# Forward and backward of four attention layers on one core: the derivative of the linear layers' feature map, recomputed on GpSimd from the kept feature map in place of being stored and loaded

## The chip, the core and the metric

One core of a Trainium2 chip runs the whole program in one launch. The metric is the time of one execution in device microseconds; the kernel before was run three times. A profile of one more execution gives, per engine, every instruction's start and length, the DMA transfers and the clock that TensorE was granted. The engines are called PE (TensorE, matmuls), PEld (its weight loads), DVE (VectorE), ACT (ScalarE), POOL (GpSimd) and SP (SyncE, which here only issues DMAs). ACT issues DMAs too, in the same in-order queue as its computing instructions.

## The reference, cut to what matters

The input x is 2048 tokens of 640 numbers in bfloat16. Four layers follow each other: linear attention (A), sliding-window attention (B, window 256), A, B, each with a layer norm ahead, a residual sum behind, 32 heads of 20 numbers, and weights wqkv (640x1920) and wo (640x640). The two A layers share their weights, and so do the two B layers. Outputs are the result and the gradients of x and of the four weights for a given grad_out.

```python
phi = lambda t: jnp.where(t > 0, t + 1, jnp.exp(t)) + 1e-6
pq, pk = phi(q), phi(k)
kv = jnp.einsum("bhsd,bhse->bhde", pk, v)
z = jnp.einsum("bhsd->bhd", pk)
num = jnp.einsum("bhqd,bhde->bhqe", pq, kv)
den = jnp.einsum("bhqd,bhd->bhq", pq, z)[..., None] + 1e-6
o = num / den
```

This is the A layer's inner part. For the backward the derivative of phi is needed: 1 where t > 0, and exp(t) elsewhere, that is min(exp(t), 1). Since phi(t) is max(t, 0) + min(exp(t), 1) + 1e-6, the same derivative can be had from phi itself as min(phi - 1e-6, 1).

## The kernel before

The tokens are cut into 16 tiles of 128 rows (TT = 16); layers are numbered 0 to 3. What the backward needs of an A layer is kept in HBM: pq and pk (phi of q and k), eq and ek (the derivatives, min(exp(t), 1)), v, o, the reciprocal denominators and the small matrix of kv.

The work goes through these stages, with about the times at which they run in the profile:

- First pass, to 120 us: layer 0's layer norm and q, k, v of every tile (`a_qkv`, lines 488 to 538). Each chunk of 320 columns is five matmuls (L448), an exponential on ACT into the tile `ee` (L516), a minimum with 1 on DVE (L517), and on DVE max(t, 1e-6) + ee into pq or pk (L520; pk lies in `gcar`). The v chunks are copied by ACT (L501) or DVE (L504). The transposes of the normalized input and of pq are done by PE (L464) and copied by ACT (L467). ACT issues the stores of pq, eq, pk, ek and v of the tile, 160 KB each (all DMAs of the forward have line 416).
- First combined pass, to about 420 us: per tile layer 0's output, layer 1 (the B layer, scores L826, exponentials L830 and L833 on ACT, masks L839 and L844 on POOL, the products with v L864, copies of q, k, v L695, reciprocal and output L871 and L872), and layer 2's k and v. ek of layer 2 is stored here.
- Second combined pass, about 460 to 745 us: layer 2's q (`late_q`, lines 542 to 569, begun at 420 us), its output, and layer 3. eq of layer 2 is stored here, by line 569.
- Backward of layer 3's attention, to about 1045 us (`B_attn_bwd`), whose order is written out by hand.
- A phase to about 1440 us (`bwd_phase(3, 2, 1)`): first a loop that ends layer 3's backward and starts layer 2's (gw L1327 and prod L1418 on POOL), then from 1235 us a loop over 16 tiles with layer 2's gradients of q, k and v (`lin_grads`, lines 1465 to 1508), its layer-norm backward (`tail`, L1309 to L1331) and the start of layer 1's (`local_dO`, with prod L1377 on POOL).
- Layer 1's attention backward to about 1780 us, then `bwd_phase(1, 0, None)` to the end, whose gradient loop over the tiles runs from 1965 to 2070 us and has no `local_dO`.

In `lin_grads` a tile's `start` issues on SP three transposing loads (dNT, pkT, vT) and the plain loads of eq and ek (L1476, through `load`, L1227; the issue itself is on L1128). Each of the two tiles has two buffers; in the phase of layers 3 and 2 ek lies in a part of `slabR`, so the profile calls it slabR there. `chunk` then does the banded matmuls (L1145) and, for q and k, DVE multiplies the PSUM result by eq or ek into dqkv (L1503), 320 columns at a time. dqkv is transposed by PE (L1167), copied by DVE (L1171) and multiplied by the weights (L1138, dw_ps); ACT copies the result (dh, L1309), DVE reduces it (L1317), ACT makes w (L1324), POOL adds the running gradient (gw, L1327), and DVE writes the new running gradient (gcar, L1329).

In the forward and in `bwd_phase` the order of the instructions of each engine is set ahead of the run by a planner (`Sched`, lines 87 to 200). Each operation is given to `op` with its engine, an assumed duration and the tiles that it reads and writes; the planner places them one after the other by when they could start by its own model, and each engine's queue is then fixed. A DMA counts with its size and a short time for the issue. So an operation that is taken out or added can change the order of others on every engine. On the chip each engine works through its queue in order and waits where an operand isn't ready.

Of the kernel before, what the change touches and what calls it, by code (L numbers as in the profile page):

```python
# [10 lines left out]
ACT = mybir.ActivationFunctionType  # L11
ALU = mybir.AluOpType
AX = mybir.AxisListType
BF = mybir.dt.bfloat16
# [188 lines left out]
class Kern:  # L203
    def __init__(self, ctx, tc, x0, A_wqkv, A_wo, B_wqkv, B_wo, grad_out, outs):
# [5 lines left out]
        D, T = self.D, self.T  # L210
# [59 lines left out]
        d = self.dram  # L270
        self.hn_d = [d.tile([T, D], BF, name=f"hn{l}") for l in range(4)]
        self.sv = {}
        for l in (0, 2):
            self.sv[l] = dict(
                pq=d.tile([T, D], BF, name=f"pq{l}"), pk=d.tile([T, D], BF, name=f"pk{l}"),
                eq=d.tile([T, D], BF, name=f"eq{l}"), ek=d.tile([T, D], BF, name=f"ek{l}"),
                v=d.tile([T, D], BF, name=f"v{l}"), o=d.tile([T, D], BF, name=f"o{l}"),
                r32=d.tile([T, self.H], F32, name=f"r32{l}"),
                mbd=d.tile([D, D + P], BF, name=f"mbd{l}"),
            )  # L280
# [53 lines left out]
    def forward(self, slabs):  # L334
# [5 lines left out]
        with ExitStack() as st:  # L340
# [36 lines left out]
            pk = g = self.g  # L377
# [32 lines left out]
            op = S.op  # L410
            dq = dict(SP=nc.sync, ACT=nc.scalar)

            def dma(eng, out, in_, size, r, w, **kw):
                def f():
                    with nc.allow_non_contiguous_dma(reason="strided layouts"):
                        dq[eng].dma_start(out=out(), in_=in_())
                op(eng, 60, f, r, w, dma=("D", size), **kw)
# [19 lines left out]
            KB = 1024  # L437
# [50 lines left out]
            def a_qkv(l, tt, hnT):  # L488
                sv = self.sv[l]
                c = {}  # L490

                def chunk(ci):
                    def f():
                        kind, c0 = "qkv"[ci // 2], ci * CW
                        o = c0 - ci // 2 * D
                        ps = R["s" if l == 0 and ci in (0, 2, 4) else "mm"].buf()
                        mm_chunk(ps, CW, [(lambda k=k: hnT.t[:, k, :], lambda k=k: wsb["Wqkv_A"][:, k, c0:c0 + CW],
                                           k == 0, k == DT - 1) for k in range(DT)], [key_of(hnT), ("Wqkv_A", ci)])
                        if kind == "v":
                            if ci == 4 and l == 0:  # L500
                                op("ACT", av(CW), lambda: nc.scalar.copy(vv[:, tt, o:o + CW], ps.t[:, 0:CW]), [ps],  # L501
                                   [("vv", tt, ci)])
                            else:
                                op("DVE", vp(CW), lambda: nc.vector.tensor_copy(vv[:, tt, o:o + CW], ps.t[:, 0:CW]),  # L504
                                   [ps], [("vv", tt, ci)])
                            if ci == 5:
                                dma("ACT", lambda: self.tm_view(sv["v"])[:, tt, :], lambda: vv[:, tt, :], 160 * KB,
                                    [("vv", tt, 4), ("vv", tt, 5)], [])
                            return
                        if ci % 2 == 0:  # L510
                            c[kind] = R["ee"].buf()
                            if kind == "q":
                                c["p"] = R["pp"].buf()
                        e = c[kind]
                        es = lambda: e.t[:, o:o + CW]
                        op("ACT", av(CW), lambda: nc.scalar.activation(es(), ps.t[:, 0:CW], ACT.Exp), [ps], [(e, ci)])  # L516
                        op("DVE", v4(CW), lambda: nc.vector.tensor_scalar(  # L517
                            out=es(), in0=es(), scalar1=1.0, scalar2=None, op0=ALU.min), [], [(e, ci)])
                        pd = (lambda: c["p"].t[:, o:o + CW]) if kind == "q" else (lambda: pk[:, tt, o:o + CW])
                        op("DVE", vp(CW), lambda: nc.vector.scalar_tensor_tensor(  # L520
                            out=pd(), in0=ps.t[:, 0:CW], scalar=1e-6, in1=es(), op0=ALU.max,
                            op1=ALU.add), [ps, (e, ci)], [(c["p"], ci) if kind == "q" else ("pk", tt, ci)])
                        if ci == 3 and "q" in c:
                            p_, e = c["p"], c["q"]
                            turn("s", lambda: pqT[:, :, tt * P:(tt + 1) * P], lambda: p_.t, DT, [(p_, 0), (p_, 1)],
                                 [("pqT", tt)])
                            dma("ACT", lambda: self.tm_view(sv["pq"])[:, tt, :], lambda: p_.t, 160 * KB,
                                [(p_, 0), (p_, 1)], [])
                            dma("ACT", lambda e=e: self.tm_view(sv["eq"])[:, tt, :], lambda e=e: e.t, 160 * KB,
                                [(e, 0), (e, 1)], [])  # L530
                        if ci == 3:
                            e = c["k"]
                            dma("ACT", lambda: self.tm_view(sv["pk"])[:, tt, :], lambda: pk[:, tt, :], 160 * KB,
                                [("pk", tt, 2), ("pk", tt, 3)], [])
                            dma("ACT", lambda e=e: self.tm_view(sv["ek"])[:, tt, :], lambda e=e: e.t, 160 * KB,
                                [(e, 2), (e, 3)], [])
                    return f
                return [chunk(ci) for ci in range(6)]

# [2 lines left out]
            def late_q(l, tt, where="s1", **F):  # L542

                sv = self.sv[l]
                q_left.discard(tt)
                e, p_ = R["ee"].buf(), R["pp"].buf()
                own = lambda: pqT[:, :, tt * P:(tt + 1) * P]
                for ci in range(2):
                    ps, c0 = R[where].buf(), ci * CW
                    for k0, k1 in ((0, 2), (2, DT)):  # L550
                        def f(ps=ps, c0=c0, k0=k0, k1=k1):
                            for k in range(k0, k1):
                                nc.tensor.matmul(ps.t[:, 0:CW], lhsT=own()[:, k, :], rhs=wsb["Wqkv_A"][:, k, c0:c0 + CW],
                                                 start=(k == 0), stop=(k == DT - 1))
                        op("PE", pe([CW] * (k1 - k0)), f, [("pqT", tt), ("Wqkv_A", ci)], [ps], **F)
                    es = lambda c0=c0: e.t[:, c0:c0 + CW]
                    op("ACT", av(CW), lambda ps=ps, es=es: nc.scalar.activation(es(), ps.t[:, 0:CW], ACT.Exp), [ps],
                       [(e, ci)], **F)
                    op("DVE", v4(CW), lambda es=es: nc.vector.tensor_scalar(out=es(), in0=es(), scalar1=1.0, scalar2=None,
                                                                            op0=ALU.min), [], [(e, ci)], **F)  # L560
                    op("DVE", vp(CW), lambda ps=ps, es=es, c0=c0: nc.vector.scalar_tensor_tensor(
                        out=p_.t[:, c0:c0 + CW], in0=ps.t[:, 0:CW], scalar=1e-6, in1=es(), op0=ALU.max, op1=ALU.add),
                       [ps, (e, ci)], [(p_, ci)], **F)
                if tt < 2:
                    turn("mm", own, lambda: p_.t, DT, [(p_, 0), (p_, 1)], [("pqT", tt)])
                else:
                    flip(own, lambda: p_.t, 160 * KB, [(p_, 0), (p_, 1)], [("pqT", tt)], **F)
                dma("ACT", lambda: self.tm_view(sv["pq"])[:, tt, :], lambda: p_.t, 160 * KB, [(p_, 0), (p_, 1)], [], **F)
                dma("ACT", lambda: self.tm_view(sv["eq"])[:, tt, :], lambda: e.t, 160 * KB, [(e, 0), (e, 1)], [], **F)

            def a_kv(l):
                sv = self.sv[l]
# [518 lines left out]
    def bwd_phase(self, lb, la, nb, ahead, raw):  # L1091
# [9 lines left out]
        with ExitStack() as st:  # L1101
# [125 lines left out]
            def load(name, src, tt):  # L1227
                b = R[name].buf()
                dma("SP", lambda: b.t, lambda: self.tm_view(src)[:, tt, :], 160 * KB, [], [b])
                return b  # L1230
# [234 lines left out]
            def lin_grads(tt, items, t0):  # L1465
# [4 lines left out]
                def start():  # L1470
                    for nm, src, size in (("dNT", self.tmp_dN, 192 * KB), ("pkT", sv["pk"], 160 * KB),
                                          ("vT", sv["v"], 160 * KB)):
                        c[nm] = b = R[nm].buf()
                        flip(lambda b=b: b.t, lambda src=src: src[row, :], size,
                             [("dNd", tt)] if nm == "dNT" else [], [b])
                    c["eq"], c["ek"] = load("eq", sv["eq"], tt), load("ek", sv["ek"], tt)  # L1476

                def chunk(kind, ci):
                    def f():
# [413 lines left out]
```

## Time and profile before

| | |
|---|---|
| three runs | 2145.37, 2146.77 and 2151.33 us, median 2146.77 |
| profiled execution | 2145.22 us, of which 2143.5 are the span from the first instruction to the last |
| mean granted TensorE clock | 0.975 of full speed |
| HBM | 109.02 MB read, 112.07 MB written |
| DMA issues of this change | eq 32 and ek 32 stores on ACT, as many loads on SP, 160 KB each |
| POOL in the gradient loop of layer 2, 1255 to 1370 us | 37.78 of 115 us busy |
| POOL in the gradient loop of layer 0, 1985 to 2070 us | 18.17 of 85 us busy |

How to read it: the busy times of an engine over the whole span are a mean over stages with different limits, so the prediction takes windows of single stages. A wait is given as "what waited <- what ended the wait". In the timeline a line gives the start, the length, the engine, the line of the kernel, the operation, what it writes and reads, and in brackets the idle time of the engine before it. ACTq and SPq are an engine's queue issuing a DMA; that is not counted as busy. "Landing" is the time at which a DMA's data has arrived.

### The profile page before, as it was taken

What the parts mean: (1) busy time and instruction counts of PE and PEld (TensorE: products, weight loads), DVE (VectorE), ACT (ScalarE), POOL (GpSimd) and SP (SyncE); (2) the same over time, 40 slices, a digit from 0 to 9 for tenths busy, and PEclk for the clock granted to TensorE, in tenths of its full rate; (3) what the DMA queues carried; (4) which work ended last, traced back from release to release, by engine and by line L of the source; (5) the groups of instructions that cost most, each with busy time, mean ns of one, the idle gap of its engine ahead of it and who ended that gap; (6) DMA issues with size and microseconds to landing.
All of it is one profiled execution on the core that took longest, in us unless ns stands there. A gap on an engine that the chain in (4) does not pass through costs nothing. (4 is left out here: it accounts for less than half of the span.)

```text
span 2143.5 us, 68024 instructions
## 1 busy us (share of the span) xinstructions
PE 2008.2 (94%) x27908; PEld 1389.2 (65%) x27908; DVE 1440.1 (67%) x2954; ACT 1203.3 (56%) x1995; POOL 879.4 (41%) x1850
## 2 busy tenths in 40 slices
PE   6879999889999899999899999999999999999999
PEld 4656666656666577777666667656777765666764
DVE  6757777567776599999634368606998984444651
ACT  3527878647888589899422233216988881221430
POOL 1015666316777456666223223204665652230210
PEclk9989999999999899999899999999999999999999
DMA  9928989469998788987987899847999998989943
GB/s 291 256 106 179 191 193 191 119 198 201 210 208 191 146 157 151 161 161 155 193 185 168 213 200 203 175 104 142 157 158 151 170 170 162 199 185 227 186 111 102
DMA packets 943687, 376.43 MB, mean 176 GB/s; under 512 B 821776, under 2 KB 923664, under 8 KB 943120
## 3 DMA queue, kind: packets, MB, share of 16 engines
q1 hardware_dynamic: 866176, 299.16, 71.9%
q10 hardware_dynamic: 77200, 72.94, 11.1%
q8 instruction: 218, 3.57, 0.7%
q14 instruction: 93, 0.76, 0.1%
HBM read 109.02 MB, written 112.07 MB: 103 GB/s over the span
## 5 line engine op out<-in xcount | busy, mean ns | idle before, releaser
L1693 DVE TENSOR_TENSOR ds_sb<-pair,e_sb 128x768 bf16<-128x768 f32 x480 | 437.6, 951 | 57.8 <-PE pair L1654 49.6
L1673 ACT ACTIVATE e_sb<-pair 128x768 bf16<-128x768 f32 x480 | 390.9, 815 | 95.6 <-PE pair L1654 67.4
L839 POOL TENSOR_SCALAR_AFFINE_SELECT e_sb<-e_sb 128x384 bf16<-128x384 bf16 (+1 forms) x512 | 198.3, 406 | 357.5 <-ACT e_sb L830 335.7
L830 ACT ACTIVATE e_sb<-s_ps 128x1152 bf16<-128x1152 f32 (+2 forms) x256 | 273.8, 1070 | 100.2 <-PE s_ps L826 78.4
L1685 POOL TENSOR_SCALAR_AFFINE_SELECT e_sb<-e_sb 128x256 bf16<-128x256 bf16 x448 | 182.0, 406 | 227.1 <-ACT e_sb L1673 226.9
L1327 POOL TENSOR_TENSOR gw<-w,gcar 128x640 f32<-128x640 f32 x64 | 89.4, 1397 | 423.4 <-ACT w L1324 406.8
L1138 PEld LDWEIGHTS <-slabR 128*128 128x128 bf16 x1920 | 185.6, 98 | 116.1 <-DMA slabR<-o 3.7
L1682 POOL TENSOR_SCALAR_AFFINE_SELECT e_sb<-e_sb 128x256 bf16<-128x256 bf16 x512 | 206.5, 406 | 89.3 <-ACT e_sb L1673 89.3
L1718 PEld LDWEIGHTS <-dsT 128*128 128x128 bf16 x2880 | 146.2, 97 | 97.7 <-issue 91.5
L1709 ACT COPY dsT<-dsT_ps 128x768 bf16<-128x768 bf16 x240 | 191.2, 796 | 9.4 <-PE dsT_ps L1706 6.6
L448 PE MATMUL mm_ps<-slabR,hnTB 128*128 128x320 bf16 x960 | 170.5, 308 | 10.5 <-DVE gcar L520 6.0
L1706 PE MATMUL dsT_ps<-ident,ds_sb 128*128 128x128 bf16 x1848 | 158.2, 223 | 1.3 <-ACT dsT L1709 1.1
L1722 PEld LDWEIGHTS <-ds_sb 128*128 128x128 bf16 x2880 | 145.1, 96 | 0.8 <-issue 0.8
L1722 PEld LDWEIGHTS <-e_sb 128*128 128x128 bf16 x2880 | 145.0, 96 | 0.0
L844 POOL TENSOR_SCALAR_AFFINE_SELECT e_sb<-e_sb 128x512 bf16<-128x512 bf16 x224 | 142.6, 636 | 0.0
L833 ACT ACTIVATE e_sb<-s_ps 128x384 bf16<-128x384 f32 (+2 forms) x256 | 119.9, 468 | 32.3 <-PE s_ps L826 15.1
L1138 PE MATMUL dw_ps<-dqkv,slabR 128*128 128x480 bf16 x640 | 134.7, 366 | 0.0
L1309 ACT ACTIVATE dh<-mm_ps 128x320 f32<-128x320 f32 x64 | 28.0, 437 | 189.8 <-PE mm_ps L1138 164.9
L1138 PE MATMUL dw_ps<-dqkv,om 128*128 128x480 bf16 x640 | 134.2, 366 | 0.0
L1654 PE MATMUL pair<-slabR 32*128 32x384 bf16 (+2 forms) x1024 | 120.5, 326 | 12.0 <-DVE ds_sb L1693 5.2
L1138 PEld LDWEIGHTS <-om 128*128 128x128 bf16 x800 | 77.5, 98 | 71.3 <-DMA om<-o 2.4
L864 PEld LDWEIGHTS <-e_sb 128*128 128x128 bf16 x2880 | 105.5, 96 | 26.6 <-POOL e_sb L844 7.5
(234 smaller groups left out, 4357.6 us busy)
## 6 DMA issues: line engine op xcount, KB each, us to landing
qkvp<-qk_slab SPq DMA_DIRECT2D x64, 256.0 KB, 3.7
hn<-slabR SPq DMA_DIRECT2D x64, 160.0 KB, 2.9
qkvp<-v_slab SPq DMA_DIRECT2D x32, 256.0 KB, 3.4
slabR<-qkvp SPq DMA_DIRECT2D x16, 512.0 KB, 4.8
o<-o SPq DMA_DIRECT2D x48, 160.0 KB, 2.9
eq<-ee ACTq DMA_DIRECT2D x32, 160.0 KB, 3.0
pq<-pp ACTq DMA_DIRECT2D x32, 160.0 KB, 2.4
ek<-ee ACTq DMA_DIRECT2D x32, 160.0 KB, 2.7
```

The costliest lines, as they stand in the source:

```text
L448: nc.tensor.matmul(ps.t[:, w0:w0 + width], lhsT=lhsT(), rhs=rhs(), start=start, stop=stop)
L830: op("ACT", av(3 * nkt * P), lambda: nc.scalar.activation(e.t[:, 0:3, 0:nkt, :], s3.t[:, :, 0:nkt * P].rearrange("p h (i q) -> p h i q", q=P),
L839: nc.gpsimd.affine_select(out=v, in_=v, compare_op=ALU.is_ge, fill=0.0, base=0, pattern=[[0, h1 - h0], [1, P]], channel_multiplier=-1)
L1138: nc.tensor.matmul(ps.t[:, w0:w0 + width], lhsT=lhsT(), rhs=rhs(), start=start, stop=stop)
L1673: nc.scalar.activation(E[n][:, 2 * p:2 * p + 2], PR[h][:, :, 0:3 * P].rearrange("p i (j q) -> p i j q", q=P), ACT.Exp, scale=self.c_att)
L1682: nc.gpsimd.affine_select(out=e[:, :, j, :], in_=e[:, :, j, :], compare_op=ALU.is_ge, fill=0.0, base=0, pattern=[[0, 2], [-1, P]], channel ...
L1685: nc.gpsimd.affine_select(out=e[:, :, j, :], in_=e[:, :, j, :], compare_op=ALU.is_ge, fill=0.0, base=-1, pattern=[[0, 2], [1, P]], channel ...
L1693: nc.vector.tensor_mul(DS[n][:, hs], PR.pop(h)[:, :, 0:3 * P].rearrange("p i (j q) -> p i j q", q=P), E[n][:, hs])
L1706: nc.tensor.transpose(ps[:, i, j, :], DS[n][:, 2 * p + i, j, :], self.ident)
L1709: (nc.scalar.copy if by == "A" else nc.vector.tensor_copy)(TSB[h], TPS.pop(h))
L1718: nc.tensor.matmul(a[:, 0, hh, :], lhsT=TSB[2 * n + hh // 2][:, hh % 2, j, :], rhs=ld[g]["K"][:, k, cs], start=(i == 0), stop=(i == len(dq ...
L1722: nc.tensor.matmul(a[:, 1 + x, hh, :], lhsT=src[n][:, hh, j, :], rhs=ld[g][rhs][:, q, cs], start=(i == 0), stop=(i == len(dkv) - 1))
```

## The change

The tensors eq and ek in HBM are gone, and with them the 64 stores of the forward (16 tiles, q and k, two layers). In the backward the tiles named eq and ek are loaded from pq and pk, and one GpSimd instruction per loaded tile (128 x 640, bfloat16) subtracts 1e-6 and takes the minimum with 1, in place; the planner is told 1000 ns for it. The forward still computes min(exp(t), 1) in `ee`, since pq and pk are made from it.

```diff
@@ Kern.__init__
-                eq=d.tile([T, D], BF, name=f"eq{l}"), ek=d.tile([T, D], BF, name=f"ek{l}"),
@@ a_qkv
                         if ci == 3 and "q" in c:
-                            p_, e = c["p"], c["q"]
+                            p_ = c["p"]
...
-                            dma("ACT", lambda e=e: self.tm_view(sv["eq"])[:, tt, :], lambda e=e: e.t, 160 * KB,
-                                [(e, 0), (e, 1)], [])
                         if ci == 3:
-                            e = c["k"]
...
-                            dma("ACT", lambda e=e: self.tm_view(sv["ek"])[:, tt, :], lambda e=e: e.t, 160 * KB,
-                                [(e, 2), (e, 3)], [])
@@ late_q
-                dma("ACT", lambda: self.tm_view(sv["eq"])[:, tt, :], lambda: e.t, 160 * KB, [(e, 0), (e, 1)], [], **F)
@@ lin_grads, start
-                    c["eq"], c["ek"] = load("eq", sv["eq"], tt), load("ek", sv["ek"], tt)
+                    for nm, p_ in (("eq", "pq"), ("ek", "pk")):
+                        c[nm] = b = load(nm, sv[p_], tt)
+                        op("POOL", 1000, lambda b=b: nc.gpsimd.tensor_scalar(
+                            out=b.t, in0=b.t, scalar1=-1e-6, scalar2=1.0, op0=ALU.add, op1=ALU.min), [], [b])
```

The planner's new queues differ from the old in these ways. In the first pass and the first combined pass the order changes on PE, DVE, ACT and SP in every tile; in the second combined pass ACT's queue loses its issues and the order is otherwise as before. In the backward the 64 new instructions stand on POOL between gw and prod, and SP's queue and the order of a few tiles at the start of the gradient loops change. The number of instructions on PE, DVE and SP is as before.

## The prediction, before the changed kernel was run

> **What bounds the kernel now.** I read the first section of the page, then each stage's engine shares (the windows), then the waits and the timeline inside the three stages that the edit touches. The page says only that TensorE is nearly full:
>
> ```profile
> span 2143.5 us, 68024 instructions
> PE 2008.2 (94%) x27908; PEld 1389.2 (65%) x27908; DVE 1440.1 (67%) x2954; ACT 1203.3 (56%) x1995; POOL 879.4 (41%) x1850
> ```
>
> 135 us of the span are not PE's, and an edit that changes no matmul can only win or lose there. The stages differ:
>
> ```profile
> 40.00:80.00 40.00, 34.11 (x296) 24.71 (x297) 30.89 (x87) 23.98 (x61) 0.00 (x0) 0.96 0.91 254
> 80.00:120.00 40.00, 34.12 (x345) 25.80 (x344) 24.69 (x73) 21.57 (x53) 0.00 (x0) 1.00 0.86 225
> 1255.00:1370.00 115.00, 108.62 (x993) 81.92 (x991) 101.31 (x215) 36.78 (x95) 37.78 (x28) 1.00 1.01 196
> 1985.00:2070.00 85.00, 84.74 (x863) 66.95 (x862) 59.73 (x142) 35.47 (x91) 18.17 (x13) 1.00 0.78 163
> ```
>
> Columns: window, its length, then busy us of PE, PEld, DVE, ACT, POOL, the granted clock, the DMA engines' share, GB/s. The forward's first pass (two upper rows) leaves PE idle 15% with the DMA engines at 0.86 to 0.91. The gradient loop of layer 2 (1255 to 1370) has DVE 88% busy. That of layer 0 (1985 to 2070) is all PE: 84.74 of 85.
>
> **Part 1, the stores that go.** 64 issues leave ScalarE's queue:
>
> ```profile
> L416 ACTq DMA_DIRECT2D eq<-ee x32: 326/422/1445, 15.0 to 654.7; - x32
> L416 ACTq DMA_DIRECT2D ek<-ee x32: 326/388/672, 23.6 to 422.8; - x32
> ```
>
> (min/median/max ns.) An issue costs nothing while the engine still executes the instruction before it. So in each stage I took ACT's busy time, and its busy time joined with the stretches in which it issues a DMA; the difference is time that only issues fill.
>
> First pass, 20 to 115 us: 53.2 busy, 72.1 joined, so 18.9 us over 73 issues; 29 of these are eq and ek, a share of 7.5 us. That such time reaches PE is seen here:
>
> ```profile
> 93.62 0.34 ACTq L416 DMA_DIRECT2D pk<-gcar  x1
> 94.00 0.67 ACTq L416 DMA_DIRECT2D ek<-ee  x1
> 94.72 0.42 ACT L501 CAST vv<-s_ps 128x320 bf16<-128x320 f32 x1 [1.70 <-DMA eq<-ee]
> ```
>
> ScalarE stood still for 1.70 us ahead of the copy that frees a PSUM bank, behind a store whose data came late and then ek's issue; PE's own largest ACT wait in this window is on that copy (4.4 us in 7 waits). In the new order the copy stands ahead of pk, and ek and eq are gone. Nine tiles from 56.3 to 110.3 us take 6.0 us each, the five before 7.1; PE's part is about 5.0 (six chunks at 0.68 from start to start, two transposes at 0.27, the sums 0.4). So at most 9x1.0 + 5x2.1 = 19.5 us are there, and at least nothing. I take **-7.5**, the issues' share.
>
> First combined pass, 165 to 420 us: 18.8 us over 98 issues, 15 of them ek: 2.9 us. But here the planner, given less to place, changes the order in every tile. PE's largest wait is "mm_ps L448 <- DVE gcar L520", 6.0 us in 8. In the tile at 289 us L520 ends at 294.62 and PE goes on at 294.68 after 0.75 idle. In the new order VectorE does the oB pair (L871 and L872, 0.74 us) and one more copy (L695, 0.44) ahead of L517 and L520, while PE has 12 pv matmuls (0.45) more to do first. Placed with the durations of these rows, rs is known at 293.14, the oB pair ends at 293.34, and L482, L695, L517 and L520 behind it end at about 294.9: 0.3 us later than now, some 4 us over 13 tiles. Ends -2.9 and +4; I take **+1.5**, nearer to the walk, since ScalarE gains slack.
>
> Between the passes, 420 to 505 us, 7 issues go where the DMA share reaches 1.06: -3 to 0, **-1**. Second combined pass, 505 to 700: same order, 14.4 us over 75 issues, 10 of them eq: -1.9 to 0; PE idles little there, **-1**. The rings' earlier release and the 10.5 MB less written (64 x 160 KB) cost nothing and are in these terms.
>
> **Part 2, the loads.** Backward, 64 loads of 160 KB go on, in SP's queue as before, only from pq and pk. pq is then read twice. **0.**
>
> **Part 3, 64 instructions on POOL**, 32 in each gradient stage, each between its load and the product L1503 that needs it. No such instruction is in the trace. Nearest rows: a select in place, one bf16 input, takes 293, 406, 520 and 636 ns for 128, 256, 384 and 512 columns, so 114 ns per 128 and 750 ns at 640. The two-input gw of 128x640 f32 takes 1397. Below: a memset of 128x128 takes 204 where the select takes 293, so perhaps 0.5 us. I take 0.75, the select being one-input and in place, and keep 0.5 to 1.4.
>
> What hides it: the time between a load's landing and its use. In layer 2's loop eq lands 4.2 to 7.8 us before L1503 in the steady tiles, ek 2.9 to 8.0. There POOL's order per tile becomes gw, prod, ek, eq. In the tile at 1283: prod ends at 1286.1, ek landed at 1284.6, done by 1286.9 (1287.5 at 1.4 us), used at 1288.4. The next eq lands at 1288.5, done by 1289.9 at worst; the next gw begins at 1292.3. Only the fill is bare: third and fourth ek, slack 1.4 and 0.7 us, which 0.75 to 1.4 overruns by 0 to 0.7 each. Queued behind the waiting op on POOL is gw, and DVE's in-order L1329 waits for gw. **+1.5** with some contention (next paragraph), ends 0 and +20.
>
> In layer 0's loop the order is gw, ek, eq, gw, and eq lands only just ahead of gw: at 2007.6, gw at 2008.25. So gw starts at 2008.35 (2009.0 at 1.4), ends by 2010.4, L1329 by 2011.3, and DVE's next work is at 2012.22: covered. At worst (eq landing at 1989.4, gw at 1988.5) L1329 is 0.2 us late. Fill: slacks 1.3 and 2.0. **+0.5**, ends 0 and +2.
>
> **POOL beside DVE.** L1329 shows what a POOL instruction does to a DVE instruction with two SBUF inputs:
>
> ```profile
> L1329 DVE SCALAR_TENSOR_TENSOR gcar<-slabR,sm,gw x14: 1945/1948/1951, 1258.9 to 1367.7; 128x640 bf16<-128x640 bf16 x14
> ```
>
> ```profile
> L1329 DVE SCALAR_TENSOR_TENSOR gcar<-hn,sm,gw x14: 873/876/884, 1984.3 to 2069.0; 128x640 bf16<-128x640 bf16 x14
> ```
>
> The upper group has POOL's prod begin beside it, the lower has POOL idle: 1.07 us of each is waiting for prod. The Trainium skill, SBUF — State Buffer, section "Who interferes with whom", calls this an exclusive lock: what issues first holds the shared port pair for its whole instruction and the other blocks. The trace agrees, with these 1948 against 876 ns. By that rule it is open whether L1329 or the new ek op, both ready when prod ends, goes first; that is rival B.
>
> **Sum** against the profiled execution's own 2145.2 us (span 2143.5 and 1.7 around it): -7.5 +1.5 -1 -1 +1.5 +0.5 = -6.0, or 2139.2. The median of the three runs, 2146.8, lies 1.6 above that execution; the sum from there is 2140.8. I forecast **2140**, between the two.
>
> **Rivals.**
> A, the stores were not what ScalarE waited for. In the first pass ACT also waits for DVE and PE (11.3 us on mv, 6.7 on pp), and the new order may cost in the combined pass what the first pass gains: 0 +4 -1 -1 +1.5 +0.5 = +4 at one end, and with a first pass that wins 4 us and the combined pass at +1.5 it is -2.5. Time 2147. For it: DVE is 62 to 77% busy there (24.69 and 30.89 of 40), in order and close behind PE. Against: the 1.70 us stall above.
> B, slower: in layer 2's loop the new ek op starts the moment prod ends, and L1329, waiting for the same ports, is blocked a second time. Each of 14 tiles is then later by the op's length: 0.75x14 = 10.5 us, at 1.4 us 19.6. DVE passes it on: after L1329 come L1380 to L1384, the dOp store on ScalarE behind them, and dh, for which PE already waits 4.3 us in 9 tiles. With the forward's gain at its middle: 2146.8 -8 +10.5 to +19.6 = 2149 to 2158, so 2154. It decides from about 1.0 us per op. Against: L1329 is waiting first, and POOL has a gap in front of each instruction; no row here shows a DVE instruction between two ready POOL instructions.
> C, that the edit does not do what it says: the order listing has 64 new POOL instructions, 64 issues fewer on ACT and as many loads as before. Excluded.
>
> **Chances.** Forecast 0.55, its own range 2129 to 2146; A 0.22; B 0.23. 0.3% (6.4 us, about what a measurement of this kernel tells from no change) lies at 2140.3 and 2153.2. The forecast lies on the first of these and its first-pass term reaches 12 us down but 7.5 up, so it splits 0.36 faster and 0.19 within; A 0.04, 0.14, 0.04; B 0.00, 0.04, 0.19. Together 0.40, 0.37, 0.23. Range 2128 to 2154: the low end is the forecast with 12 us more of the first pass's 19.5, the high end takes in B to its middle.
>
> **What would show it.** First pass: tiles of about 5.5 us from 56 us on, and vv L501 no longer behind an issue. Combined pass: the idle time on gcar L520, 0.75 us a tile now, at about 1.0. New POOL group: x64, near 750 ns. L1329 in layer 2's loop: 1948 as now; 2.7 to 3.3 us would be B. Layer 0's loop: PE 84.7 of 85 as now. I am wrong if the first pass ends no earlier than now, if the new op is above 1.4 us, or if one of the combined passes grows by more than 5 us.

## The result, and the profile after

The changed kernel takes 2168.87 us (median of four runs, 2167.95 to 2172.16) where the kernel before takes 2146.07 in the same session: a ratio of 1.0109, 95% interval 1.0082 to 1.0137. It is 23 us slower; the forecast was 2140, and the range ended at 2154. The first section of its page has the cause in one number:

```profile
span 2167.0 us, 67954 instructions
PE 2013.4 (93%) x27908; PEld 1389.9 (64%) x27908; DVE 1441.3 (67%) x2954; ACT 1206.6 (56%) x1995; POOL 1043.8 (48%) x1914
```

POOL has 64 instructions more and is busy 164.4 us longer (879.4 before), 2.57 us for each; the prediction had 0.75. The groups of instructions, by shape, name them (busy us, mean ns, idle time before them):

```profile
L1471 POOL TENSOR_SCALAR eq<-eq 128x640 bf16<-128x640 bf16 x32 | 78.0, 2438 | 21.8 <-DMA eq<-pq 9.6 <-DVE dz L1446 6.3 <-PE mm_ps L1131 3.8
L1471 POOL TENSOR_SCALAR slabR<-slabR 128x640 bf16<-128x640 bf16 x16 | 42.8, 2674 | 17.9 <-DMA slabR<-pk 16.6
L1471 POOL TENSOR_SCALAR ek<-ek 128x640 bf16<-128x640 bf16 x16 | 42.1, 2631 | 25.5 <-DMA ek<-pk 23.7 <-DVE gcar L1322 1.1
```

(Lines of the changed kernel are 1 to 7 below those of before in the places named here: gw is L1320, gcar L1322, the product L1499, and slabR is ek of layer 2.) The same four windows as in the prediction:

```profile
40.00:80.00 40.00, 37.97 (x350) 27.82 (x349) 33.47 (x99) 28.01 (x67) 0.00 (x0) 1.00 1.11 251
80.00:120.00 40.00, 34.06 (x327) 25.01 (x325) 24.82 (x75) 17.49 (x41) 0.00 (x0) 0.89 0.46 150
1255.00:1370.00 115.00, 104.18 (x948) 77.74 (x946) 96.21 (x205) 35.15 (x92) 98.96 (x51) 1.00 0.89 188
1985.00:2070.00 85.00, 77.60 (x781) 60.86 (x779) 53.34 (x124) 31.62 (x81) 73.06 (x34) 1.00 0.81 168
```

The first pass is better (PE 37.97 of 40 where it had 34.11). Both gradient loops are worse: POOL goes from 37.78 to 98.96 us in layer 2's and from 18.17 to 73.06 in layer 0's, and PE falls from 84.74 to 77.60 in the latter (whose window now begins 13 us ahead of the loop's first gw and so takes in its fill). The timeline of POOL there shows why (start, length, operation, idle time before it in brackets):

```profile
2007.38 1.40 POOL L1320 TENSOR_TENSOR gw<-w,gcar 128x640 f32<-128x640 f32 x1
2008.87 3.04 POOL L1471 TENSOR_SCALAR ek<-ek 128x640 bf16<-128x640 bf16 x1
2011.98 2.35 POOL L1471 TENSOR_SCALAR eq<-eq 128x640 bf16<-128x640 bf16 x1
2014.41 1.40 POOL L1320 TENSOR_TENSOR gw<-w,gcar 128x640 f32<-128x640 f32 x1
2016.44 2.49 POOL L1471 TENSOR_SCALAR ek<-ek 128x640 bf16<-128x640 bf16 x1 [0.63 <-DMA ek<-pk]
2019.01 2.35 POOL L1471 TENSOR_SCALAR eq<-eq 128x640 bf16<-128x640 bf16 x1
2021.44 1.40 POOL L1320 TENSOR_TENSOR gw<-w,gcar 128x640 f32<-128x640 f32 x1
```

From the first gw to the second 7.03 us pass, and no bracket stands between them: 1.40 + 3.04 + 2.35 and three gaps of 0.08. The tile took 6.57 us before, set by PE. In the next tile ek first waits 0.63 us for its load, is lengthened less, and the tile again takes 7.03. The two kinds alternate through the loop: in every second tile ek waits 0.6 to 1.2 us. POOL has become the bound, with the loads close behind it. In layer 2's loop POOL nearly is the bound:

```profile
1335.54 1.40 POOL L1320 TENSOR_TENSOR gw<-w,gcar 128x640 f32<-128x640 f32 x1 [0.49 <-ACT w L1317]
1336.89 1.35 POOL L1370 TENSOR_TENSOR prod<-slab,o 128x640 f32<-128x640 bf16 x1
1338.32 2.80 POOL L1471 TENSOR_SCALAR slabR<-slabR 128x640 bf16<-128x640 bf16 x1
1341.20 2.35 POOL L1471 TENSOR_SCALAR eq<-eq 128x640 bf16<-128x640 bf16 x1
```

Here the tile takes 8.50 us, 8.2 before, with 0.49 idle. A third loss lies at the start of layer 2's stage, on DVE:

```profile
1075.59 0.82 DVE L1413 TENSOR_REDUCE dd<-prod 128x32 f32<-128x640 f32 x1 [6.17 <-POOL prod L1411]
```

Three of the new instructions (1066.19 to 1074.1) stand ahead of the first prod on POOL. DVE waits 6.17 us for it, the next gw is late, and the gap between the second and third gw grows from 15.8 to 21.5 us.

Where the 23 us lie, from the starts of matmuls and gw instructions in the two traces: the forward ends 3.25 us earlier; layer 2's stage (first gw to the next attention's first matmul) takes 416.8 us for 403.1, +13.7; layer 0's (first gw to the last instruction) 364.3 for 354.6, +9.7. The attention stages and what lies around them, which the change does not touch, add 3.3. One of them (layer 3's, from the first to the last of its score matmuls, L1654 of the kernel before) takes from 310.2 to 319.0 us in the profiled executions, so below the two gradient stages are compared by themselves.

### The profile page after: what moved, and what is told of

It is laid out like the page before. It is cut to its first block, busy times and chain, and to the rows that moved or that the text cites. A ratio compares the mean times of both kernels' runs of the same rounds, so it can differ in the third digit from the quotient of the medians.

```text
span 2167.0 us, 67954 instructions
## 1 busy us (share of the span) xinstructions
PE 2013.4 (93%) x27908; PEld 1389.9 (64%) x27908; DVE 1441.3 (67%) x2954; ACT 1206.6 (56%) x1995; POOL 1043.8 (48%) x1914
## 5 line engine op out<-in xcount | busy, mean ns | idle before, releaser
L1320 POOL TENSOR_TENSOR gw<-w,gcar 128x640 f32<-128x640 f32 x64 | 89.5, 1398 | 224.1 <-ACT w L1317 214.7
L857 PE MATMUL pv_ps<-v_slab,e_sb 128*128 128x32 bf16 x2880 | 117.1, 177 | 8.6 <-POOL e_sb L837 8.0
```

The source lines that it names most:

```text
L857: nc.tensor.matmul(pv.t[:, h % 16, :], lhsT=e.t[:, hh, j, :], rhs=vts[j].t[:, h, :], start=(j == 0), stop=(j == nkt - 1))
```

## The experiments

Theory P: the POOL instruction takes about 2.6 us and not 0.75, and POOL's in-order queue then holds up gw and prod. Its rivals: the loads or the new order of the issues (F), a wait for the derivative rather than the queue (W), a loss in plain proportion to POOL's added time (L). For the forward: theory O, the planner's new order spoils the first combined pass, against S, that pass swallows a gain anyway. Summary, with the length of the POOL instruction (mean ns), the last attention matmul of the forward and the two gradient stages against the kernel before (720.4 and 757.6 us in the profiled executions), and the ratio of the times to the kernel before, run beside it:

| kernel | POOL ns | forward | gradients | ratio (95%) |
|---|---|---|---|---|
| changed kernel | 2545 | -3.3 | +23.4 | 1.0109 (1.0082 to 1.0137) |
| e1, no instruction | - | -4.2 | +1.7 | 1.0006 (0.9990 to 1.0022) |
| e2, before + instruction | 2524 | -0.9 | +22.5 | 1.0113 (1.0090 to 1.0137) |
| e4, min in the product | - | -2.7 | 0.0 | 0.9992 (0.9977 to 1.0006) |
| e8, select | 836 | -3.0 | +1.4 | 1.0010 (0.9995 to 1.0026) |
| e9, half the columns | 1439 | +1.4 | +9.8 | 1.0021 (1.0002 to 1.0040) |
| e3, one step | 1938 | -2.8 | +17.0 | 1.0059 (1.0025 to 1.0093) |
| e10, planner told 2500 | 2616 | -3.3 | +18.8 | 1.0072 (1.0048 to 1.0095) |
| e12, on a spare tile | 2500 | -2.2 | +16.2 | 1.0076 (1.0050 to 1.0102) |
| e6, e4 + all entries kept | - | -13.1 | +1.9 | 0.9963 (0.9945 to 0.9982) |
| e7, e4 + layer 2's entries | - | -11.5 | +0.1 | 0.9950 (0.9932 to 0.9969) |
| e11, changed + layer 2's entries | 2551 | -14.9 | +25.0 | 1.0048 (1.0029 to 1.0068) |

The three columns in the middle come from one profiled execution of each kernel. Those of e8 (2156.11 us) and e9 (2161.72) are the slowest of ten, and that of e3 (2168.68) lies 7 us above its median, so for these three the ratio is the better measure.

**e1, the instruction left out**, and with it the derivative.

```diff
                         c[nm] = b = load(nm, sv[p_], tt)
-                        op("POOL", 1000, lambda b=b: nc.gpsimd.tensor_scalar(
-                            out=b.t, in0=b.t, scalar1=-1e-6, scalar2=1.0, op0=ALU.add, op1=ALU.min), [], [b])
```

> The 64 POOL instructions are left out (the gradients are multiplied by the loaded feature map itself, so the derivative is left out); the stores stay away and the loads stay on pq and pk. Theory P (each POOL instruction takes about 2.6 us, and POOL, in order, then gives gw and the derivative late): the forward stays as in the changed kernel (last attention matmul near 717), the backward falls back to the lengths of the kernel before, so 2143 us (2140 to 2146). Rival F (the loss comes from the loads or from the new order of the issues, not from POOL's instruction): 2160 or more. Rival Q (half of each): about 2155.

Measured 2149.78 us beside 2147.25, ratio 1.0006. The gradient stages are back (+1.7), the forward is as in the changed kernel. F falls. The time lies 4 us above P's range: the forward's 4 us do not show in the median.

**e2, the instruction alone**, on the loaded eq and ek of the kernel before.

```diff
-                    c["eq"], c["ek"] = load("eq", sv["eq"], tt), load("ek", sv["ek"], tt)
+                    for nm in ("eq", "ek"):
+                        c[nm] = b = load(nm, sv[nm], tt)
+                        op("POOL", 1000, lambda b=b: nc.gpsimd.tensor_scalar(
+                            out=b.t, in0=b.t, scalar1=-1e-6, scalar2=1.0, op0=ALU.add, op1=ALU.min), [], [b])
```

> The kernel before, with all its stores and loads of eq and ek, and the same 64 POOL instructions added on the loaded tiles. Theory P: the forward ends as before (720.4), the two gradient stages lose the 14 and 9.5 us that the changed kernel loses, so 2146 + 23 = 2169 us (2165 to 2173), and the instruction has the same 2.3 to 3.0 us. Rival F: 2146 to 2150, as the kernel before.

Measured 2173.31, ratio 1.0113, gradients +22.5: all of the loss, with no store taken away. With e1 this settles which part of the change costs the time.

**e5, what the instruction takes, by form**, on a scratch tile in the first pass, where POOL has nothing else to do (four of each):

```diff
+                both = dict(scalar1=-1e-6, scalar2=1.0, op0=ALU.add, op1=ALU.min)
+                one = dict(scalar1=1.0, scalar2=None, op0=ALU.min)
...
+                    for _ in range(4):
+                        op("POOL", dur, f, [], [e])
```

> The kernel before, with 32 POOL instructions on a scratch tile at the start of the forward, four of each form, where POOL has no other work. Theory P1 (POOL's cost of a tensor_scalar is by step and element): two steps on 128x640 bf16 take 2.35 us, one step about 1.2 to 1.4, 320 columns 1.2, 128 columns 0.55, and the f32 tile as much as the bf16. Theory P2 (by instruction and element, whatever the steps): one step also 2.35. Under both the select of 640 columns takes 0.75 us, as read off the rows of 128 to 512, so that it was the wrong neighbour. Rival X (the length is contention with VectorE in the gradient loops alone): two steps take 0.75 to 1.4 here.

A single execution, 2155.43 us. The groups, by shape:

```profile
L993 POOL TENSOR_SCALAR e_sb<-e_sb 128x640 f32<-128x640 f32 x4 | 9.4, 2348 | 0.3
L991 POOL TENSOR_SCALAR e_sb<-e_sb 128x640 bf16<-128x640 bf16 x4 | 9.4, 2347 | 0.3
L992 POOL TENSOR_SCALAR e_sb<-e_sb 128x640 bf16<-128x640 bf16 x4 | 7.2, 1807 | 0.3
L996 POOL TENSOR_TENSOR e_sb<-e_sb 128x640 bf16<-128x640 bf16 x4 | 5.6, 1393 | 0.3
L994 POOL TENSOR_SCALAR e_sb<-e_sb 128x320 bf16<-128x320 bf16 x4 | 5.1, 1280 | 0.3
L999 POOL COPY e_sb<-e_sb 128x640 bf16<-128x640 bf16 x4 | 2.9, 719 | 0.2
L997 POOL TENSOR_SCALAR_AFFINE_SELECT e_sb<-e_sb 128x640 bf16<-128x640 bf16 x4 | 2.9, 718 | 0.3
L995 POOL TENSOR_SCALAR e_sb<-e_sb 128x128 bf16<-128x128 bf16 x4 | 2.6, 654 | 0.3
```

Two steps (L991) take 2347 ns with nothing to wait for, so X falls. One step (L992) takes 1807: neither P1's half nor P2's whole. The first step costs most and the second 0.54 us. The type does not matter (f32 2348); the columns do, at 3.3 ns each ((2347 - 1280)/320). The select that the prediction extrapolated takes 718 ns, near the 750 read off its row, and a copy takes as much. The row was read rightly and belonged to another kind of instruction: even two inputs (1393 for the product of bf16 tiles, 1397 for gw's of f32 tiles) are cheaper than one input with a scalar. The Trainium skill, GPSIMD Engine Reference, section "Engine selection", calls one-input work on GpSimd "roughly line-rate" and two-input work about twice as slow as on VectorE. The copy and the product stand in that order here, 719 and 1393 ns, and the instruction with scalars does not fit it, at 1807 and 2347.

**e8, e9, e3: the same place at other prices.** Each replaces the instruction: by a select that keeps every element (e8, which leaves the derivative out), by the same on half the columns (e9, which leaves it out in the other half), by one step (e3, without the subtraction of 1e-6).

```diff
-                        op("POOL", 1000, lambda b=b: nc.gpsimd.tensor_scalar(
-                            out=b.t, in0=b.t, scalar1=-1e-6, scalar2=1.0, op0=ALU.add, op1=ALU.min), [], [b])
+e8                      op("POOL", 1000, lambda b=b: nc.gpsimd.affine_select(
+                            out=b.t, in_=b.t, compare_op=ALU.is_ge, fill=0.0, base=D, pattern=[[-1, D]],
+                            channel_multiplier=0), [], [b])
+e9                      ... out=b.t[:, 0:CW], in0=b.t[:, 0:CW], scalar1=-1e-6, scalar2=1.0, op0=ALU.add, op1=ALU.min
+e3                      ... out=b.t, in0=b.t, scalar1=1.0, scalar2=None, op0=ALU.min
```

> The changed kernel with the POOL instruction replaced by a select of the same tile that keeps every element (0.72 us each; the derivative is left out), so that part 3 of the prediction is tried at the price that it assumed. Theory P (only the price was wrong): the backward costs 0 to 3 us more than without any POOL instruction, so 2150 (2147 to 2153). Rival L (every us that POOL adds is paid in proportion, 22 us for 2.5 us each): 6 us more, 2155 or above. Rival B of the prediction (a second blocking of VectorE's last addition in layer 2's loop): 0.72 us in each of 14 tiles, 10 us more, 2159, with that addition at 2.7 us.

> The changed kernel with the POOL instruction on the first 320 of 640 columns only (1.28 us each instead of 2.35; the derivative is left out in the others). Theory P (POOL's queue is the loss, and it appears only when gw, prod and two of these no longer fit a tile): layer 2's loop needs 1.4 + 1.4 + 2.6 = 5.4 us of 8.2 and layer 0's 4.0 of 6.6, so little is left of the loss: 2151 (2148 to 2155). Rival L (in proportion): half of the 22 us, 2159.

> The changed kernel with one step in the POOL instruction instead of two (min with 1; the subtraction of 1e-6 is left out): 1.81 us each by the forms run, some 2.0 beside VectorE. Theory P (POOL's queue, by the sum of a tile): layer 0's loop needs 1.4 + 2 x 1.9 + 0.2 = 5.4 us of 6.6 and layer 2's 6.8 of 8.2, so both keep their pace and only the fills are paid, 3 to 6 us over the run without the instruction: 2154 (2151 to 2158). Rival L (in proportion to the length): 0.75 of the 22 us, 2164.

Measured 2152.23, 2153.41 and 2161.50 us; against the kernel before (2149.44 for the first two, 2147.11 for e3) ratios of 1.0010, 1.0021 and 1.0059. The instruction takes 0.84, 1.44 and 1.94 us in them on average (the select 0.72 where it is not lengthened). e8 and e9 lie in P's ranges and under the 2155 and 2159 of L; e3 lies above P's range and under L's 2164. In e8 the gradient stages lose 1.4, near the prediction's own +2.0. Of the 9.8 us in e9's trace, 4.5 lie between the two loops of layer 2's stage, where PE waits for loads and e1 loses 3.2 without any such instruction; the loops and fills lose 5. By the ratios, e8, e9, e3 and the changed kernel cost 0.9, 3.2, 11.4 and 22.1 us more than e1, each uncertain by 5 to 8. In proportion to the length, 7, 12.5 and 17 would stand in place of the first three. So little is paid up to 1.44 us and most of the loss comes above it; L falls at the short lengths and is open at 1.94. There P's sum per tile fails as well: it left POOL idle time and forecast 3 to 6 us over e1.

The trace of e3 shows what the sum leaves out. In its layer 0 loop the gaps from gw to gw alternate between 5.9 and 7.8 us (6.57 before), and in every second tile the ek instruction stands waiting at the head of POOL's queue, with gw behind it. Most of these waits end with the landing of its load (1.92 us at 2031.24, 2.96 at 2060.19). e9 has such waits too (2.85 us at 2027.88). Why the loads land late in every second tile was not tried.

**e12, the queue without the data.** The product takes min itself (as e4), and the 64 instructions work on a spare tile in the same places of POOL's queue:

```diff
+                        op("POOL", 1000, lambda: nc.gpsimd.tensor_scalar(
+                            out=spare, in0=spare, scalar1=-1e-6, scalar2=1.0, op0=ALU.add, op1=ALU.min),
+                           [b], ["spare"])
...
```

> The run with min in VectorE's product, and besides it the 64 two-step POOL instructions on a spare tile, in the same places of POOL's queue as in the changed kernel: they wait for no load and nobody waits for them, so only their time in the queue is left. Theory P (they hold up gw and prod, which stand behind them): layer 0's loop stays near 7.0 us a tile, since 1.4 + 2 x 2.6 us fill it, layer 2's near 8.4, the fills cost less than the 5.7 and 3.7 us of the changed kernel, and the time is 2160 (2156 to 2166). Rival W (the product's wait for the derivative, and POOL's wait for the loads, are the loss): the time of the run with min in the product, 2147.

Measured 2165.72 us, ratio 1.0076; gradients +16.2 of 23.4. W falls as the main cause: time in the queue alone brings back the fill of layer 2's stage (+5.7, to the tenth), that of layer 0's (9.5 us between the first two gw, as in the changed kernel, 5.7 before) and most of layer 2's loop. But P is wrong on layer 0's loop, which returns to 6.57 us a tile:

```profile
2041.37 1.40 POOL L1322 TENSOR_TENSOR gw<-w,gcar 128x640 f32<-128x640 f32 x1 [0.31 <-ACT w L1319]
2042.85 4.77 POOL L1473 TENSOR_SCALAR spare<-spare 128x640 bf16<-128x640 bf16 x2
2047.94 1.40 POOL L1322 TENSOR_TENSOR gw<-w,gcar 128x640 f32<-128x640 f32 x1 [0.32 <-ACT w L1319]
```

Both instructions take 2.35 here (4.77 for two with the gap), 0.31 us are left over, and PE sets the pace. In the changed kernel the first of the pair takes 3.04, and in every second tile it waits for its load instead. e12 takes away both; the trace of e10, below, tells them apart.

**e10, the planner told the price.**

```diff
-                        op("POOL", 1000, ...
+                        op("POOL", 2500, ...
```

> The changed kernel, but the planner is told 2500 ns for the POOL instruction instead of 1000. Theory P (length): one prod moves ahead of the third instruction at the start of layer 2's stage, which takes 2 to 3 us off its fill; layer 0's loop stays at 7.0 us a tile, since POOL is full there in any order: 2164 (2161 to 2168). Rival R (a bad order from a wrong cost is the whole loss): back to 2150.

Measured 2164.64 us, ratio 1.0072. The extra wait in the fill of layer 2's stage goes (15.4 us between the second and third gw, 15.8 before), but the stage's second loop takes 3.7 us longer than in the changed kernel. Layer 0's loop stays at 7.0 a tile, as P had it. R falls: the wrong cost in the plan is 4.6 of the 23.4 us in the gradient stages. In this order no instruction waits for a load in seven tiles in a row, from 2012.37 to 2061.58 us, and each still takes 7.03:

```profile
2047.52 1.40 POOL L1320 TENSOR_TENSOR gw<-w,gcar 128x640 f32<-128x640 f32 x1
2049.00 3.04 POOL L1471 TENSOR_SCALAR eq<-eq 128x640 bf16<-128x640 bf16 x1
2052.12 2.35 POOL L1471 TENSOR_SCALAR ek<-ek 128x640 bf16<-128x640 bf16 x1
2054.55 1.40 POOL L1320 TENSOR_TENSOR gw<-w,gcar 128x640 f32<-128x640 f32 x1
```

So the 0.69 us by which the first of the pair is lengthened are enough to make POOL overflow; the waits for loads are not needed for it.

**e4, the derivative inside the product**, on DVE, with no instruction of its own and without the subtraction of 1e-6:

```diff
-op("DVE", dve_ns(CW), lambda: nc.vector.tensor_mul(dst(), ps.t[:, 0:CW], e.t[:, e0:e0 + CW]), [ps, e]
+op("DVE", dve_ns(CW), lambda: nc.vector.scalar_tensor_tensor(
+    out=dst(), in0=e.t[:, e0:e0 + CW], scalar=1.0, in1=ps.t[:, 0:CW], op0=ALU.min, op1=ALU.mult), [ps, e]
```

> The changed kernel without the POOL instruction; VectorE's product takes min(pq, 1) times the PSUM chunk in one two-step instruction, reading the loaded pq or pk (the subtraction of 1e-6 is left out). Theory P: the product stays near 480 ns, since it is bound by its PSUM input, and the time is that of the run without the POOL instruction, 2143 us (2139 to 2146). Rival D (the two-step form is slower than the plain product, as its 876 ns for 640 columns against 480 for 320 leaves open): with 0.1 us more in each of 128 products, up to 6 us more in layer 2's loop, where VectorE is 88% busy: 2150.

Measured 2146.74 us beside 2147.25, ratio 0.9992. The product's groups:

```profile
L1497 DVE SCALAR_TENSOR_TENSOR dqkv<-eq,mm_ps 128x320 bf16<-128x320 bf16 x64 | 29.2, 479 | 9.7 <-PE mm_ps L1138 9.7
L1497 DVE SCALAR_TENSOR_TENSOR dqkv<-ek,mm_ps 128x320 bf16<-128x320 bf16 x32 | 14.3, 483 | 0.0
```

480 ns, as the plain product: D falls, and the gradient stages are those of the kernel before. What is left to explain is the forward, 2.7 us earlier instead of 8.

**e6 and e7, the order kept.** On top of e4 the planner is given empty entries where the stores stood, which emit nothing; in e7 those of layer 2 alone.

```diff
                         if ci == 3 and "q" in c:
+                            op("ACT", 60, lambda: None, [(c["q"], 0), (c["q"], 1)], [], dma=("D", 160 * KB))
...
                         if ci == 3:
+                            op("ACT", 60, lambda: None, [(c["k"], 2), (c["k"], 3)], [], dma=("D", 160 * KB))
...
```

> As the run with min in the product, but the planner still sees the 64 stores that are gone (empty entries with a store's cost and data, which emit nothing), so that every engine of the forward keeps the order of the kernel before, less the issues. Theory O (the gain of the first pass is lost again in the first combined pass because the planner, given less to place, orders that pass worse): the first pass ends some 7 us earlier than in the kernel before, and the combined pass keeps it, so the forward ends 5 to 9 us earlier and the time is 2140 (2137 to 2143). Rival S (the combined pass swallows a gain whatever its order, since another engine or the clock sets it): the forward ends 2 to 4 us earlier as in the changed kernel, and the time is 2146.

> The same, but with empty entries for the stores of layer 2 alone (those in the combined passes); the first pass is planned without them, as in the changed kernel. Theory O: the first pass ends 11 us earlier as in the changed kernel, the combined pass gives back at most 3, so the forward ends 8 to 11 us earlier and the time is 2138 (2135 to 2141). Rival S: 2146. If the order of the first pass, and not that of the combined pass, were what spoils the latter: 2146 here and 2140 in the run with all entries.

Measured 2141.30 and 2139.32 us beside 2149.44: 0.9963 and 0.9950, both intervals under 1. O is shown and S falls. The first attention matmul (the first product with v) comes 8.3 (e6), 10.4 (e7) and 11.0 us (changed kernel) earlier than before; 244 us on, at the same matmul of the end of the first combined pass, they stand at -7.4, -9.5 and +2.3. The changed kernel's order gives back 13 us in that pass. PE's waits in it (165 to 395 us; us, times, longest), first the kernel before, then the changed one, then e7:

```profile
PE mm_ps L448 <- DVE gcar L520: 6.0, 8, 0.8
PE s_ps L826 <- ACT e_sb L830: 2.1, 5, 1.3
PE pv_ps L864 <- POOL e_sb L844: 1.8, 4, 1.0
```

```profile
PE s_ps L819 <- ACT e_sb L823: 11.5, 11, 2.2
PE pv_ps L857 <- POOL e_sb L837: 5.7, 14, 1.1
...
PE mm_ps L447 <- DVE gcar L519: 0.2, 1, 0.2
```

```profile
PE mm_ps L447 <- DVE gcar L519: 7.2, 10, 0.8
PE pv_ps L862 <- POOL e_sb L842: 2.9, 5, 1.1
PE s_ps L824 <- ACT e_sb L828: 1.8, 2, 1.6
```

In the new order the wait on gcar that the prediction followed is gone (0.2 us); in its place PE waits 11.5 us for the exponentials of the scores and 5.7 for the masks behind them. With the old order they are back at 1.8 and 2.9. Between the two matmuls named above, PE is idle 24 us in the changed kernel and 16 in the kernel before, so its waits are 8 of the 13 us; the other 5 are in longer records of the same 3852 matmuls, and why these are longer is not shown.

**e11, both together**: the changed kernel with e7's entries.

> The changed kernel with its POOL instruction, and with the empty planner entries for layer 2's stores, so that the first combined pass is ordered as in the kernel before. Theories O and P together: the two faults add up, so the forward ends 11 us earlier than in the kernel before and the backward loses 22: 2160 (2157 to 2163), 8 to 10 under the changed kernel. If the earlier forward were lost again in the backward: 2168.

Measured 2156.87 us, ratio 1.0048: the forward is 14.9 us earlier, the gradients 25.0 later. The two faults add up.

Two versions beat both kernels, e6 and e7, and their intervals overlap. The faster median is e7's: the stores gone, pq and pk loaded, min(pq, 1) taken in the product, and the combined passes planned as if the stores were there.

## Why the prediction was wrong

- **Part 3, the price of the POOL instruction, is the term that failed**: 0.75 us with ends 0.5 and 1.4, measured 2.35 alone and 2.55 in place. Both ends came from other kinds of instruction. The text said itself that above 1.4 it would be wrong. Near its own price its working held: e8, at 0.84 us on average, lost 1.4 for a predicted 2.0.
- **The fills.** "Only the fill is bare" was right in kind and small in size: it counted the third and fourth ek, and left out that the first prod queues behind three of the new instructions (5.7 us) and that layer 0's second gw queues behind three of them as well (3.8).
- **Layer 2's and layer 0's loops.** 1.5 and 0.5 us were taken; measured +13.7 and +9.7 for the stages, fills included. Of the 13.7, 5.7 are the first fill, 5.3 the loop over the tiles and most of the rest lies between them; of the 9.7, 8.3 are the loop with its fill. For layer 0's the prediction's worst case was +2: at 1.4 us POOL's sum of a tile is 4.2 of 6.57, where it is 1.40 + 2 x 2.35 and the lengthening, 7.03 with the gaps.
- **Rival B fell in its mechanism, not its sign.** L1322 in layer 2's loop has a median of 1947 ns, as before: it goes ahead, and it is the POOL instruction beside it, which starts 0.08 us after prod ends, that is longer (2.80).
- **First pass, -7.5: right in its sign, and too small.** The changed kernel's first attention matmul comes 11.0 us earlier. With the old order (e6) the last copy of the normalized tile comes 8.0 us earlier (110.27 to 102.26), near the issues' share of the prediction; the changed kernel's own order takes 5.6 more there, which the prediction had in its range but not in its sum. PE's window shows the gain, 34.11 to 37.97 of 40. e6 takes away the issues and the 160 KB that each moves together, so that ScalarE's time and not the traffic is the gain is not shown.
- **First combined pass, +1.5 with an end of +4: wrong**, measured +13. The walk through one tile followed the one wait that stood out, and that wait did shrink; what came late next, the scores' exponentials, was not looked for in the other tiles.
- **Between the passes -1, second combined pass -1**: -4.1 (392 to 494 us) and -1.4 measured. **Loads 0**: e4's gradient stages equal those of before.
- Sum: the forward -3.3 instead of -8.0, the backward +23.4 instead of +2.0. The forward is this near only because its errors partly cancel: 3.5 and 3.1 us better in the first pass and between the passes, nearly 12 worse in the combined pass.

## What to carry to other kernels

A price for an instruction that no row shows is not bounded by rows of another kind on the same engine, however near in shape: here one input with two scalar steps costs 1.7 times the two-input product and 3.3 times the select, and the step that looks like a detail is better folded into an instruction that already reads the tile. Sum an in-order engine's whole tile against the tile's time with the price doubled, count what queues behind the first instructions of a stage, and look at which of its instructions can stand waiting for a load with others behind them. Where a planner sets the order, a saving is worth only what the new order leaves of it: here giving the planner the old entries kept 9 us (0.9950 against 0.9992) that the plan without them lost.

## What the runs showed of the hardware that was not expected

A tensor_scalar on POOL takes about 0.22 us and 3.3 ns for each column with two steps (from 654, 1280 and 2347 ns at 128, 320 and 640), 128x640 in 2347 ns, for bf16 and f32 alike.

The POOL instruction and DVE's two-input addition slow each other down in different measure by who starts when. Just behind gw both start together, DVE's 0.05 us ahead of the POOL instruction of 2008.87 shown above:

```profile
2008.82 0.88 DVE L1322 SCALAR_TENSOR_TENSOR gcar<-hn,sm,gw 128x640 bf16<-128x640 bf16 x1 [3.73 <-POOL gw L1320]
```

L1322 keeps its 0.88 us and the POOL instruction takes 3.04 instead of 2.35. In e12 the POOL instruction starts at 2042.85, and DVE's addition follows from 2043.09:

```profile
2043.09 1.15 DVE L1324 SCALAR_TENSOR_TENSOR gcar<-hn,sm,gw 128x640 bf16<-128x640 bf16 x1
```

It takes 1.15 and ends while the POOL instruction, 2.35 long and not lengthened, still runs. The Trainium skill, SBUF — State Buffer, section "Who interferes with whom", calls the port pair that the two engines share "an exclusive lock" and says that issue order decides who blocks. The first case agrees in who yields; in the second the one that came later was slowed by 0.27 us and not blocked for the 2.1 us that were left.
